# All matmuls at full 128x128 shape, and Q and K loaded four tokens per partition, in an attention and gated-unit kernel

## The chip, the cores and the metric

The kernel runs on one core of one Trainium2 chip. The metric is device time in microseconds (us) of one execution, lower is better. A core has a matrix engine (TensorE, PE in the profile, with its weight loads shown apart as PEld), a vector engine (VectorE, DVE), a scalar engine for activations (ScalarE, ACT), a general engine (GpSimd, POOL) and a queue engine that issues transfers (SyncE, SP). Each engine runs its own instructions in order; semaphores tie the engines together. SBUF is the on-chip memory, PSUM the memory that TensorE writes to.

## What is computed

Causal attention with a decay bias over 8 batches, 8 heads, 576 tokens and 64 dimensions a head, followed by a gated linear unit whose gate is a causal convolution of five taps.

```python
B, H, S, D = q.shape                                   # 8, 8, 576, 64
cum  = np.cumsum(np.maximum(s, 0.0), axis=-1)
bias = -(cum[:, :, :, None] - cum[:, :, None, :])
scores = np.matmul(q, k.transpose(0, 1, 3, 2)) / sqrt(D) + np.minimum(bias, 0.0)   # causal mask
attn = softmax(scores)
x = np.matmul(attn, v)                                 # to [B, S, 512]
gate = sigmoid(sum(conv_w[k] * x_shifted[k] for k in range(5)))
out = (gate * (x @ w_val)) @ w_out
```

## The kernel before

The bias splits into a factor per query, which the softmax normalisation cancels, and a factor per key, `w = exp(cum - half)`. It is multiplied into V, and a 65th column of V holds `w` itself, so that the same matmul also gives the softmax denominator. No maximum is subtracted. A small check on the denominators at the end decides whether a slower general path runs; with these inputs it doesn't.

576 tokens are four blocks of 128 and a tail block of 64 (`kbs`, `kbo`). Work goes by steps n: step n belongs to batch b = n / 4 and head pair p = n % 4, and a loop over n emits, with delays of one step or more, everything else:

- `load(b+1)` (L264), emitted at the first step of a batch: 15 transfers from HBM, for each token block Q, K and V in turn, every one in pieces of one token's 64 values (256 bytes). POOL casts Q and K to bf16 (L274) and multiplies V by `w` (L279, L281).
- `qk_transpose` (L286): five TensorE transposes of a 128-column slice into PSUM, the last of 64 tokens, and one DVE copy out (L294) to `QT` or `KT`, in which two heads lie one above the other, 64 partitions each.
- `scores4` (L296) and `scores` (L318): matmuls with 64 rows, one for each head, on partitions 0 to 63 and 64 to 127. ACT takes the exponential (L329), DVE masks the diagonal blocks (L332).
- `av` (L335): per head pair 30 matmuls of 65 columns; those for the tail queries have 64 columns of weights, those with the tail keys 64 rows. Two PSUM tiles, `psA` and `psB`, each evacuated by a reciprocal and a multiplication on DVE (L355, L356).
- `x_transpose` and `conv` (L360, L372): the result is transposed back (L368), copied by DVE (L370), and the five taps are one ACT instruction (L376), four DVE instructions (L378) and a tanh (L381).
- `val` and `outp` (L384, L397): the two products of the gated unit, four matmuls each, evacuated by DVE (L394) and ACT (L405).

A scheduler at build time puts the emitted instructions into an order for each engine, so that matmuls of different kinds stand mixed on TensorE. All transposes and both products of the gated unit share two PSUM buffers named `m` (pool `ps_m`); the scores have two of their own (`ps`). `qkst` and `vst` are the staging buffers of the transfers, four of each.

Of the kernel before, what the change touches and what calls it, by code (L numbers as in the profile page):

```python
# [206 lines left out]
def pcol(kb, qb):
    return DIAG[kb] if kb == qb else OFF0[kb] + kbo[qb]


def main_path(ctx, tc, q, k, v, s, moe_w_val, moe_conv_w, moe_w_out, out, okcnt):


    nc = tc.nc
# [34 lines left out]
    for i in range(NKB):  # L249
        n = kbs[i]  # L250
        pt = ps_m.tile([n, 64], FP32, name="m")
        nc.tensor.transpose(pt, cum[:, kbo[i]:kbo[i] + n], identf[0:64, 0:64])
        nc.scalar.activation(out=w[0:n, i, :], in_=pt, func=AF.Exp)

    recs = const_p.tile([128, B, 4, NKB, 2], FP32, name="recs")
    nc.vector.memset(recs, 1.0)
    psA = ps_av.tile([128, 3, 2, 65], FP32, name="psA")
    psB = ps_av.tile([128, 2, 2, 65], FP32, name="psB")
    nc.vector.memset(psB, 1.0)
# [4 lines left out]
    def load(b):  # L264
        qb_t = qkb_p.tile([128, NKB, 512], BF16, name="qb")
        kb_t = qkb_p.tile([128, NKB, 512], BF16, name="kb")
        Vp = v_p.tile([128, NKB, 8, 65], BF16, name="Vp")
        for i in range(NKB):
            n = kbs[i]
            for src, dst in ((q, qb_t), (k, kb_t)):  # L270
                st = stage_p.tile([128, 512], FP32, name="qkst")
                nc.sync.dma_start(out=st[0:n, :].rearrange("s (h d) -> s h d", h=8),
                                  in_=src[b, :, kbo[i]:kbo[i] + n, :].rearrange("h s d -> s h d"))
                nc.gpsimd.tensor_copy(dst[0:n, i, :], st[0:n, :])  # L274
            st = stage_p.tile([128, 512], FP32, name="vst")
            nc.sync.dma_start(out=st[0:n, :].rearrange("s (h d) -> s h d", h=8),
                              in_=v[b, :, kbo[i]:kbo[i] + n, :].rearrange("h s d -> s h d"))
            wb = w[0:n, i, b * 8:(b + 1) * 8]
            nc.gpsimd.tensor_tensor(Vp[0:n, i, :, 0:64], st[0:n, :].rearrange("s (h d) -> s h d", h=8),  # L279
                                    wb.unsqueeze(2).to_broadcast([n, 8, 64]), ALU.mult)  # L280
            nc.gpsimd.tensor_copy(Vp[0:n, i, :, 64:65], wb.unsqueeze(2))  # L281
        QT = qkt_p.tile([128, 4, S], BF16, name="QT")
        KT = qkt_p.tile([128, 4, S], BF16, name="KT")
        stage[b] = dict(qb=qb_t, kb=kb_t, Vp=Vp, QT=QT, KT=KT)

    def qk_transpose(b, p, which):  # L286
        st = stage[b]
        src, dst = (st["qb"], st["QT"]) if which == 0 else (st["kb"], st["KT"])
        pt = ps_m.tile([128, S], BF16, name="m")
        for i in range(NKB):  # L290
            n = kbs[i]
            nc.tensor.transpose(pt[:, kbo[i]:kbo[i] + n], src[0:n, i, p * 128:(p + 1) * 128],  # L292
                                ident[0:n, 0:n])
# [234 lines left out]
```

## Time and profile before

| | us |
|---|---|
| median of 3 runs | 349.25 |
| fastest and slowest of them | 346.63, 351.47 |
| the profiled execution | 348.8 |
| its span, first to last instruction | 347.2 |
| outside the span | 1.6 |

All durations are from the one profiled execution, so sums are made against its span of 347.2 us and the 1.6 us around it. An instruction group's line gives its source line, engine, operation, output and inputs by the program's names, shapes and count; behind the first bar the busy time and the mean duration of one in ns; behind the second the idle time of the engine just before, and who ended it. A matmul's shape is written rows*columns of the array that it uses, then the size of its streamed operand.

### The profile page before, as it was taken

How to read it: one execution, taken by the hardware profiler on the slowest of the kernel's cores; microseconds unless marked ns; L12 is line 12 of the kernel's file. 1: busy time of each engine (PE TensorE's matmuls, PEld its weight loads, DVE VectorE, ACT ScalarE, POOL GpSimd, SP SyncE). 2: the span in 40 equal slices, each digit the busy share in tenths (PEclk: the TensorE clock that was granted, in tenths of full speed). 3: DMA queues.
4: the chain of work that ended last, by engine and by line, in shares of the span. 5: the costliest groups of instructions: out<-in, count | busy, mean ns of one | idle time of the engine just before them, and what ended most of it. 6: DMA issues, size and time to landing. Idle time of an engine off the chain costs nothing.

```text
span 347.2 us, 6219 instructions
## 1 busy us (share of the span) xinstructions
PE 270.9 (78%) x2439; PEld 161.2 (46%) x2439; DVE 244.8 (70%) x466; ACT 168.7 (49%) x222; POOL 125.0 (36%) x179
## 2 busy tenths in 40 slices
PE   0236984878688798879997989889887998993990
PEld 0123652456345464556455535465554455561440
DVE  3023432774698789986989797968988789989740
ACT  0215740664248346932676263835484548741630
POOL 3661418760874017460558073803670000000000
PEclk9999999999999789955996798658995799696797
DMA  6995979971797007960499049912860030030322
GB/s 124 202 234 151 212 127 162 219 127 29 146 197 127 2 10 195 208 135 2 154 218 190 16 153 203 176 18 70 208 90 0 30 108 2 6 132 0 115 83 86
DMA packets 121910, 40.50 MB, mean 117 GB/s; under 512 B 116176, under 2 KB 116176, under 8 KB 121872
## 3 DMA queue, kind: packets, MB, share of 16 engines
q1 hardware_dynamic: 118992, 40.00, 56.6%
q10 hardware_dynamic: 2880, 0.01, 0.5%
q8 instruction: 21, 0.34, 0.5%
q14 instruction: 17, 0.14, 0.1%
HBM read 30.57 MB, written 9.44 MB: 115 GB/s over the span
## 4 chain that ended last, share of the span: by engine, by line
PE 41%; DVE 34%; ACT 10%; DMA 6%; issue 3%; POOL 3%; ACTq 1%; DVEq 0%; POOLq 0%
DVE gp L378 21%; PE m L392 9%; PE psB L349 8%; PE m L292 7%; PE ps L327 6%; ACT P L329 6%; PE psA L349 4%; DVE P L332 4%; PE m L368 4%; DMA cwT<-in_moe_conv_w_dram 3%; DVE glu L394 3%; PE m L402 2%; DVE xn L356 2%; DVE QT L294 1%; ACT gp L376 1%
## 5 line engine op out<-in xcount | busy, mean ns | idle before, releaser
L378 DVE SCALAR_TENSOR_TENSOR gp<-xT,cwT,gp 128x576 f32<-128x576 bf16 x128 | 118.0, 926 | 5.3 <-ACT gp L376 5.0
L329 ACT ACTIVATE P<-ps 128x1024 bf16<-128x1024 f32 x96 | 95.7, 1025 | 48.9 <-PE ps L327 48.6
L349 PEld LDWEIGHTS <-P 128*128 128x128 bf16 (+2 forms) x960 | 57.6, 118 | 37.2 <-issue 16.9
L327 PE MATMUL ps<-QT,KT 64*128 64x128 bf16 (+4 forms) x512 | 62.0, 297 | 12.8 <-ACT P L329 11.6
L279 POOL TENSOR_TENSOR Vp<-vst,w 128x512 bf16<-128x512 f32 (+1 forms) x40 | 52.9, 1322 | 28.0 <-DMA vst<-in_v_dram 21.3
L392 PE MATMUL m<-xT,wv 128*128 128x288 bf16 x256 | 51.0, 347 | 8.9 <-DVE xT L370 6.2
L349 PE MATMUL psB<-Vp,P 128*128 128x65 bf16 (+2 forms) x576 | 53.2, 226 | 5.3 <-DVE xn L356 3.9
L381 ACT ACTIVATE th<-gp 128x576 f32<-128x576 f32 x32 | 21.9, 684 | 48.4 <-DVE glu L394 48.2
L402 PE MATMUL m<-wo,glu 128*128 128x512 bf16 (+1 forms) x160 | 39.7, 389 | 0.2
L274 POOL CAST qb<-qkst 128x512 bf16<-128x512 f32 (+1 forms) x40 | 31.1, 779 | 21.6 <-DMA qkst<-in_q_dram 20.9
L392 PEld LDWEIGHTS <-wv 128*128 128x128 bf16 x256 | 26.4, 114 | 22.4 <-issue 12.3
L274 POOL CAST kb<-qkst 128x512 bf16<-128x512 f32 (+1 forms) x40 | 30.7, 769 | 16.1 <-DMA qkst<-in_k_dram 16.1
L294 DVE COPY QT<-m 128x576 bf16<-128x576 bf16 x32 | 14.5, 455 | 31.1 <-PE m L292 31.0
L327 PEld LDWEIGHTS <-KT 64*128 64x128 bf16 x512 | 24.5, 104 | 25.9 <-issue 18.7
L394 DVE SCALAR_TENSOR_TENSOR glu<-th,m 128x288 bf16<-128x288 f32 x64 | 28.7, 450 | 10.9 <-PE m L392 10.5
L376 ACT ACTIVATE gp<-xT,cwT 128x576 f32<-128x576 bf16 x32 | 24.9, 778 | 21.3 <-DVE xT L370 20.9
L292 PE MATMUL m<-ident,qb 128*128 128x128 bf16 (+1 forms) x160 | 24.2, 258 | 12.8 <-POOL qb L274 10.2
L405 ACT COPY ot<-m 128x512 f32<-128x512 f32 (+1 forms) x40 | 22.9, 583 | 22.8 <-PE m L402 20.4
L349 PE MATMUL psA<-Vp,P 128*128 128x65 bf16 x384 | 29.0, 220 | 5.2 <-DVE xn L356 2.2
L332 DVE TENSOR_TENSOR P<-P,tri 128x1024 bf16<-128x1024 bf16 x32 | 27.6, 861 | 2.0 <-ACT P L329 1.9
L292 PE MATMUL m<-ident,kb 128*128 128x128 bf16 (+1 forms) x160 | 23.8, 252 | 6.3 <-POOL kb L274 4.0
L368 PE MATMUL m<-ident,xn 128*128 128x128 bf16 (+1 forms) x160 | 20.7, 254 | 5.5 <-DVE QT L294 4.4
(45 smaller groups left out, 175.4 us busy)
## 6 DMA issues: line engine op xcount, KB each, us to landing
qkst<-in_q_dram SPq DMA_DIRECT2D x32, 256.0 KB, 4.6
qkst<-in_k_dram SPq DMA_DIRECT2D x32, 256.0 KB, 4.9
vst<-in_v_dram SPq DMA_DIRECT2D x32, 256.0 KB, 4.8
out_dram<-ot SPq DMA_DIRECT2D x32, 256.0 KB, 2.1
qkst<-in_q_dram SPq DMA_DIRECT2D x8, 128.0 KB, 5.1
qkst<-in_k_dram SPq DMA_DIRECT2D x8, 128.0 KB, 4.7
vst<-in_v_dram SPq DMA_DIRECT2D x8, 128.0 KB, 4.7
qkst<-in_moe_w_val_dram SPq DMA_DIRECT2D x4, 256.0 KB, 3.7
```

Of the source, the lines that this page charges most:

```text
L274: nc.gpsimd.tensor_copy(dst[0:n, i, :], st[0:n, :])
L279: nc.gpsimd.tensor_tensor(Vp[0:n, i, :, 0:64], st[0:n, :].rearrange("s (h d) -> s h d", h=8), wb.unsqueeze(2).to_broadcast([n, 8, 64]), AL ...
L292: nc.tensor.transpose(pt[:, kbo[i]:kbo[i] + n], src[0:n, i, p * 128:(p + 1) * 128], ident[0:n, 0:n])
L327: nc.tensor.matmul(ps[:, hh, c0:c0 + nq], st["KT"][r, p, kbo[kb]:kbo[kb] + 128], st["QT"][r, p, q0:q0 + nq], start=True, stop=True)
L329: nc.scalar.activation(out=Pt[:, :, step * 512:(step + 1) * 512], in_=ps, func=AF.Exp, scale=0.125)
L332: nc.vector.tensor_tensor(dg, dg, tri.unsqueeze(1).unsqueeze(1).to_broadcast([128, 2, 4, 128]), ALU.mult)
L349: nc.tensor.matmul(ps[0:nq, j, hh, :], lhsT, Vp[0:n, kb, 2 * p + hh, :], start=(kb == 0), stop=(kb == qb))
L368: nc.tensor.transpose(pt[:, kbo[i]:kbo[i] + n], st["xn"][0:n, i, p * 128:(p + 1) * 128], ident[0:n, 0:n])
L378: nc.vector.scalar_tensor_tensor(gp, xc[:, kk:kk + S], cwT[:, c * 5 + kk:c * 5 + kk + 1], gp, ALU.mult, ALU.add)
L392: nc.tensor.matmul(psv, wv[:, dc, c * 128:(c + 1) * 128], st["xT"][:, dc, 4 + o:4 + o + 288], start=(dc == 0), stop=(dc == 3))
L394: nc.vector.scalar_tensor_tensor(st["glu"][:, c, o:o + 288], st["th", c][:, o:o + 288], 1.0, psv, ALU.add, ALU.mult)
L402: nc.tensor.matmul(pso, st["glu"][:, c, kbo[i]:kbo[i] + nq], wo[:, c, :], start=(c == 0), stop=(c == 3))
```

## The change

Every matmul uses the full 128x128 array. The Q of two heads is kept in two tiles `QZ`, each zero in the other head's 64 partitions, so that both heads use the same 128-partition K slice as weights. The tail block of 64 tokens becomes a window of 128 (tokens 448 to 575): weights, score columns and the masked `P4` are arranged so that the first 64 rows add nothing, and only the last 64 are stored.

The first 512 tokens of Q and K come in one transfer a batch each (two for the first batch), with four successive tokens of a head on one partition, so that a piece is 1,024 bytes; the last 64 tokens of both come as a `tail` tile. The transposes then give tokens in the order (token mod 4, token / 4). K is put back in order when ACT copies it out of PSUM. Q is permuted within each 128-block by two DVE copies of 64 partitions; its order stays interleaved through the scores and the second matmul, and the DVE copy after `x_transpose` puts it back. `psA` and `psB` become one tile `psav` with one reciprocal and one multiplication for both heads.

The emission order changes too: `load_qk(b+2)` stands after the last step of batch b, V is loaded after the first, `x_transpose` and `conv` come ahead of the transposes of the next batch, `val` is two items, and the output products are spread over four steps.

```diff
 def load_qk(b):                                    # was: load(b)
+        for r, src in ((slice(0, 64), q), (slice(64, 128), k)):
+            nc.sync.dma_start(out=tail[r, :].rearrange("s (h d) -> s h d", h=8),
+                              in_=src[b, :, 512:576, :].rearrange("h s d -> s h d"))
+        nc.gpsimd.tensor_copy(tailb, tail)
...
+        parts = [(0, 2), (2, 8)] if b == 0 else [(0, 8)]
+        for h0, h1 in parts:
+            for src, f, t in ((q, qf, qb), (k, kf, kb)):
+                nc.sync.dma_start(out=f[:, h0:h1, :],
+                                  in_=src[b, h0:h1, 0:512, :].rearrange("h (p j) d -> p h (j d)", j=4))
+                nc.gpsimd.tensor_copy(
+                    t.rearrange("p j (h d) -> p h j d", h=8)[:, h0:h1],
+                    f.rearrange("p h (j d) -> p h j d", j=4)[:, h0:h1])
...
+        if which == 0:
+            for hh in range(2):
+                r = slice(64 * hh, 64 * hh + 64)
+                nc.vector.tensor_copy(st["QZ"][hh][r, p, 0:512].rearrange("d (i j r) -> d j i r", j=4, i=4),
+                                      pt[r, :].rearrange("d (j i r) -> d j i r", j=4, i=4))
+        else:
+            nc.scalar.copy(st["KT"][:, p, 0:512].rearrange("d (x j) -> d x j", j=4),
+                           pt.rearrange("d (j x) -> d x j", j=4))
-        nc.vector.tensor_copy(dst[:, p, :], pt)
...
-                r = slice(64 * hh, 64 * hh + 64)
-                nc.tensor.matmul(ps[:, hh, c0:c0 + nq], st["KT"][r, p, kbo[kb]:kbo[kb] + 128],
-                                 st["QT"][r, p, q0:q0 + nq], start=True, stop=True)
+                nc.tensor.matmul(ps[:, hh, c0:c0 + nq], st["KT"][:, p, kbo[kb]:kbo[kb] + 128],
+                                 st["QZ"][hh][:, p, q0:q0 + nq], start=True, stop=True)
...
+        pv = psav[:, :, 0:325].rearrange("t h (g d) -> t h g d", d=65)
+        rec = recs[:, b * 4 + p]
+        nc.vector.reciprocal(rec, pv[:, :, :, 64])
...
-        nc.vector.tensor_copy(st["xT"][:, p, 4:4 + S], pt)
+        nc.vector.tensor_copy(
+            st["xT"][:, p, 4:516].rearrange("d (i r j) -> d i r j", i=4, j=4),
+            pt[:, 0:512].rearrange("d (i j r) -> d i r j", i=4, j=4))
+        nc.vector.tensor_copy(st["xT"][:, p, 516:4 + S], pt[:, 512:S])
...
+        nc.gpsimd.memset(d["QZ"][0][64:128], 0.0)
+        nc.gpsimd.memset(d["QZ"][1][0:64], 0.0)
+        nc.gpsimd.memset(d["P4"], 0.0)
...
-        for c in range(4):
-            wt = stage_p.tile([128, DM], FP32, name="qkst")
-            nc.sync.dma_start(out=wt, in_=src[c * 128:(c + 1) * 128, :])
+        wt = qkf_p.tile([128, 4, DM], FP32, name="qkf")
+        nc.sync.dma_start(out=wt, in_=src.rearrange("(c p) d -> p c d", c=4))
```

The queue of SyncE at the program's start, before: transfers of Q, K and V of the first batch in turn, block by block (`qkst`, `vst`), then the weights.

```order
L243 DMA sp<-in_s_dram 64x576
L272 DMA qkst<-in_q_dram 128x8x64
L272 DMA qkst<-in_k_dram 128x8x64
L276 DMA vst<-in_v_dram 128x8x64
L272 DMA qkst<-in_q_dram 128x8x64
...
L276 DMA vst<-in_v_dram 64x8x64
L415 DMA qkst<-in_moe_w_val_dram 128x512 x4
```

The same place now; `qkf` is the staging tile of Q and K, with three buffers that the weights share.

```order
L301 DMA tail<-in_q_dram 64x8x64
L301 DMA tail<-in_k_dram 64x8x64
L312 DMA qkf<-in_q_dram 128x2x256
L312 DMA qkf<-in_k_dram 128x2x256
L312 DMA qkf<-in_q_dram 128x6x256
L312 DMA qkf<-in_k_dram 128x6x256
L323 DMA vst<-in_v_dram 128x8x64 x4
L323 DMA vst<-in_v_dram 64x8x64
L463 DMA qkf<-in_moe_w_val_dram 128x4x512
```

All of Q and K of the first batch now stands ahead of its V, and the weights behind both as before.

VectorE where the first convolution begins, before: `QT` and `KT` are copies for the second batch, `xT` and `gp` belong to the first batch's convolution.

```order
L294 COPY QT<-m 128x576 x2
L294 COPY KT<-m 128x576 x2
L294 COPY QT<-m 128x576
L294 COPY KT<-m 128x576
L370 COPY xT<-m 128x576
L294 COPY QT<-m 128x576
L294 COPY KT<-m 128x576
L378 SCALAR_TENSOR_TENSOR gp<-xT,cwT,gp 128x576
```

The same place now, with the two half-tiles of Q by their numbers.

```order
L350 COPY QZ_157<-m 64x4x4x32
L350 COPY QZ_158<-m 64x4x4x32
L403 RECIPROCAL recs<-psav 128x10
L404 TENSOR_TENSOR xn<-psav,recs 128x2x5x64
L416 COPY xT<-m 128x512
L419 COPY xT<-m 128x64
L350 COPY QZ_157<-m 64x4x4x32
L350 COPY QZ_158<-m 64x4x4x32
L427 SCALAR_TENSOR_TENSOR gp<-xT,cwT,gp 128x576
```

The K copies are gone from this engine, each Q copy is two, the copy of `xT` is two; the first `gp` still stands behind three of the four Q copies of the second batch.

## Rows read from the trace of the kernel before

**Rows 1.** The page's busy times: engine, busy us, share of the span, instructions.
```profile
PE 270.9 (78%) x2439; PEld 161.2 (46%) x2439; DVE 244.8 (70%) x466; ACT 168.7 (49%) x222; POOL 125.0 (36%) x179
```

**Rows 2.** Busy time by stage: stretch, length, engines with counts, granted clock, DMA share, GB/s.
```profile
0.00:26.00 26.00, 5.88 (x33) 3.23 (x33) 4.90 (x11) 3.45 (x8) 14.44 (x39) 1.00 0.99 186
26.00:64.00 38.00, 29.05 (x266) 17.65 (x264) 14.01 (x33) 15.98 (x20) 15.73 (x25) 1.00 0.87 168
125.00:298.00 173.00, 153.15 (x1432) 90.27 (x1433) 147.97 (x272) 100.05 (x130) 66.28 (x83) 0.81 0.52 110
```

**Rows 3.** Busy time by stage, single stretches of 20 us, same columns.
```profile
220.00:240.00 20.00, 18.97 (x161) 11.46 (x161) 16.39 (x31) 9.60 (x13) 8.08 (x9) 0.59 0.31 62
300.00:320.00 20.00, 14.19 (x129) 8.68 (x130) 18.72 (x40) 6.85 (x11) 0.00 (x0) 0.84 0.17 60
```

**Rows 4.** The end of the program, all engines in order of time.
```profile
333.83 1.02 DVE L394 SCALAR_TENSOR_TENSOR glu<-th,m 128x288 bf16<-128x288 f32 x2 [0.17 <-PE m L392]
334.34 4.61 PE L402 MATMUL m<-wo,glu 128*128 128x512 bf16 x20
```

**Rows 5.** TensorE in order of time, at a granted clock of 1.00.
```profile
196.29 0.23 PE L327 MATMUL ps<-QT,KT 64*128 64x128 bf16 x2
196.45 0.53 PE L368 MATMUL m<-ident,xn 128*128 128x128 bf16 x5
...
197.47 1.15 PE L392 MATMUL m<-xT,wv 128*128 128x288 bf16 x8
```

**Rows 6.** TensorE in order of time, at a granted clock of 0.50.
```profile
186.97 0.61 PE L327 MATMUL ps<-QT,KT 64*128 64x448 bf16 x4
...
192.03 2.08 PE L392 MATMUL m<-xT,wv 128*128 128x288 bf16 x8 [0.49 <-DVE xT L370]
```

**Rows 7.** Instruction groups of VectorE, by shape, whole span.
```profile
L378 DVE SCALAR_TENSOR_TENSOR gp<-xT,cwT,gp 128x576 f32<-128x576 bf16 x128 | 118.0, 926 | 5.3 <-ACT gp L376 5.0
L332 DVE TENSOR_TENSOR P<-P,tri 128x1024 bf16<-128x1024 bf16 x32 | 27.6, 861 | 2.0 <-ACT P L329 1.9
L356 DVE TENSOR_TENSOR xn<-psA,recs 128x384 bf16<-128x384 f32 x32 | 17.6, 551 | 0.3
L294 DVE COPY QT<-m 128x576 bf16<-128x576 bf16 x32 | 14.5, 455 | 31.1 <-PE m L292 31.0
L356 DVE TENSOR_TENSOR xn<-psB,recs 128x256 bf16<-128x256 f32 x32 | 13.3, 417 | 0.3
L355 DVE RECIPROCAL recs<-psA 128x6 f32<-128x6 f32 x32 | 6.0, 188 | 12.1 <-PE psA L349 12.1
L355 DVE RECIPROCAL recs<-psB 128x4 f32<-128x4 f32 x32 | 5.5, 172 | 6.6 <-PE psB L349 6.5
```

**Rows 8.** Instruction groups of VectorE from 298 to 347 us, where POOL is idle.
```profile
L378 DVE SCALAR_TENSOR_TENSOR gp<-xT,cwT,gp 128x576 f32<-128x576 bf16 x24 | 19.5, 815 | 2.5 <-ACT gp L376 2.3
L332 DVE TENSOR_TENSOR P<-P,tri 128x1024 bf16<-128x1024 bf16 x2 | 1.4, 687 | 0.0
```

**Rows 9.** Instruction groups of POOL, by shape, whole span.
```profile
L279 POOL TENSOR_TENSOR Vp<-vst,w 128x512 bf16<-128x512 f32 x32 | 42.6, 1331 | 27.7 <-DMA vst<-in_v_dram 21.3 <-issue 3.4 <-PE psB L349 1.9
L274 POOL CAST qb<-qkst 128x512 bf16<-128x512 f32 x32 | 24.3, 758 | 21.6 <-DMA qkst<-in_q_dram 20.9
L364 POOL MEMSET xT<- 128x16 bf16 x8 | 0.8, 110 | 62.4 <-issue 24.1 <-ACT P L329 19.5 <-PE m L392 18.8
masks.py:197 POOL MEMSET ident<- 128x128 bf16 x1 | 0.2, 205 | 0.3 <-POOLq L512 0.3
```

**Rows 10.** The start, in order of time: first cast on POOL, two exponentials of the first batch.
```profile
5.30 0.89 POOL L274 CAST qb<-qkst 128x512 bf16<-128x512 f32 x1 [3.50 <-DMA qkst<-in_q_dram]
...
30.77 1.01 ACT L329 ACTIVATE P<-ps 128x1024 bf16<-128x1024 f32 x1
...
47.95 1.02 ACT L329 ACTIVATE P<-ps 128x1024 bf16<-128x1024 f32 x1 [1.11 <-PE ps L327]
```

**Rows 11.** The line of `gp`: count, shortest, median and longest ns, first and last start.
```profile
L378 DVE SCALAR_TENSOR_TENSOR gp<-xT,cwT,gp x128: 773/814/1852, 64.5 to 330.1; 128x576 f32<-128x576 bf16 x128
```

More of the change, by code (lines that the diff above doesn't have):

```diff
@@ L249, in main_path @@
     for i in range(NKB):
[L250 to L259, printed above, removed]
-    stage = {}
@@ L264, in load @@
[L264 to L267, printed above, removed]
+        pt = ps_m.tile([128, 64], FP32, name="m")
+        nc.tensor.transpose(pt, cum[:, WIN[i]:WIN[i] + 128], identf[0:64, 0:64])
+        nc.scalar.activation(out=w[:, i, :], in_=pt, func=AF.Exp)
+    recs = const_p.tile([128, B * 4, 2, NKB], FP32, name="recs")
+    psav = ps_av.tile([128, 2, 512], FP32, name="psav")
@@ L268, in load, with load_v @@
+    def load_v(b):
+        Vp = sets[b % 2]["Vp"]
         for i in range(NKB):
             n = kbs[i]
[L270 to L275, printed above, removed]
@@ L283, in load, with tail_transpose @@
-        KT = qkt_p.tile([128, 4, S], BF16, name="KT")
-        stage[b] = dict(qb=qb_t, kb=kb_t, Vp=Vp, QT=QT, KT=KT)
+            nc.sync.dma_start(out=vst[128 - n:128, i, :, 0:64],
+                              in_=v[b, :, kbo[i]:kbo[i] + n, :].rearrange("h s d -> s h d"))
+            nc.gpsimd.tensor_tensor(Vp[:, i], vst[:, i],
+                                    w[:, i, b * 8:(b + 1) * 8].unsqueeze(2).to_broadcast([128, 8, 65]),
+                                    ALU.mult)
+    def tail_transpose(b):
+        st = stage[b]
+        pt = ps_m.tile([128, 4, 128], BF16, name="m")
+        for p in range(4):
+            nc.tensor.transpose(pt[:, p, :], st["tail"][:, p * 128:(p + 1) * 128], ident)
+        for hh in range(2):
+            r = slice(64 * hh, 64 * hh + 64)
+            nc.vector.tensor_copy(st["QZ"][hh][r, :, 512:S], pt[r, :, 0:64])
+        nc.scalar.copy(st["KT"][:, :, 512:S], pt[:, :, 64:128])
@@ L286, in qk_transpose @@
     def qk_transpose(b, p, which):
         st = stage[b]
[L288 to L293, printed above, removed]
-        nc.vector.tensor_copy(dst[:, p, :], pt)
+        c = slice(p * 128, (p + 1) * 128)
+        pt = ps_m.tile([128, 512], BF16, name="m")
@@ new lines, in qk_transpose @@
+        for j in range(4):
+            nc.tensor.transpose(pt[:, j * 128:(j + 1) * 128], st["qk"][which][:, j, c], ident)
+        if which == 0:
+            for hh in range(2):
+                r = slice(64 * hh, 64 * hh + 64)
+                nc.vector.tensor_copy(st["QZ"][hh][r, p, 0:512].rearrange("d (i j r) -> d j i r", j=4, i=4),
[3 more added lines that the diff above has]
+                           pt.rearrange("d (j x) -> d x j", j=4))
@@ L424, in main_path @@
         qk_transpose(0, p, 1)
+    load_qk(1)
     NS = B * 4
-    for n in range(NS + 9):
+    OUTS = [(0, 1), (2,), (3,), (4,)]
+    for n in range(NS + 12):
         b, p = divmod(n, 4)
-        if p == 0 and b + 1 < B:
-            load(b + 1)
         fill = []
```

183 lines of the change are left out of this document (102 added, 81 removed), and 6 rows, old and new, of the table STEPS.

## The prediction

> **What bounds the kernel now.** I read the page's busy times first, then the same by stage, then the groups of the engine that looks fullest, then a few stretches of TensorE in order of time. No engine is full over the span: PE is busy 270.9 us of 347.2, DVE 244.8 [rows 1]. The stages tell more [rows 2]. Up to 64 us the transfers bound: the DMA share is 0.99 and then 0.87, DVE has worked only 4.90 + 14.01 us, and the first `gp`, the convolution that makes up nearly half of DVE's work, starts at 64.5 [rows 11]. From 125 to 298 us two engines are nearly full at once: PE 153.15 of 173 us (88.5%), DVE 147.97 (85.5%). At the end DVE is alone, 18.72 of 20 us [rows 3]; its last `glu` ends at 334.85, then come twenty matmuls, copies and stores up to 347.2, 12.3 us [rows 4].
>
> So three things can change the time: when DVE gets its main work, how much work it has, and how often it waits for PE. I take DVE's work as the bound and ask for these three.
>
> **PE: what goes, what comes.** A change of array shape costs TensorE time. At full clock the pair of 64*128 matmuls at 196.29 is followed by the next shape 0.16 us later [rows 5], though 128 columns stream in 0.055 us: the eight matmuls of 288 columns in 1.15 us give about 0.123 us each [rows 5]. I call a change 0.1 us. Per head pair the code has some 16 of them: two around each of the three transposes' short fifth block, two around each of three score groups, four in the tail of `av`; the scheduler's mixing adds some, and following the matmul starts through the trace I count 570. That is 57 us of PE, all of which goes.
>
> In return the two heads no longer share the array. At half clock, four matmuls of 448, 448, 64 and 64 columns take 0.61 us [rows 6]. One after another, 1024 columns at 1.2 GHz would be 0.85 us, as pairs 0.43 us and the last one's run out: they run as pairs. After the change each group streams all 1024, and a head pair has three such groups: 1536 columns more, times 32, is 49,000, 20.5 us at 2.4 GHz. In the trace 180 of 288 possible pairs run together, so the loss lies between 13 and 21 us; I take 16. PE thus loses about 40 of its 271 us. It is a partner of DVE in the middle, so this is no saving in itself; it lets DVE wait less.
>
> Here a rule of the Trainium skill speaks against the change: TensorEngine Tiling (Array Packing), sections Theoretical Speedup and Performance Considerations, holds that a contraction of 64 should use two row tiles, worth up to twice the speed. The pairs above agree with it. By that rule alone the change would add 20 us to PE and save nothing. The same page says under Key Properties that a change of tiling mode drains the engine; the 0.16 us step agrees, and in this mixed order that side is the larger.
>
> **DVE: the work.** Removed, 32 of each [rows 7]: copies of QT, KT and xT (0.455 each, 1.365), two reciprocals (0.360), two multiplications for `xn` (0.968), together 2.69 us, 86.1 us. Added:
> - 64 copies of Q, 512 elements on 64 partitions, runs of 32. Bounds: 0.40, the QT row scaled to 512 elements, and 0.685, the rate of the `xn` rows (551 - 417 for 128 elements is 1.047 ns each; 417 + 256 x 1.047). Source, type and unit step are those of the QT row, so I take 0.43: 27.5 us (25.6 to 43.8).
> - 32 copies of xT, 512 elements read with a step of 32, and 32 of 64 elements. No row reads PSUM so. Same bounds; I take the upper one, 0.685, because the step is unlike the QT row, and 0.19 for the short one as for a reciprocal: 28.0 us (18 to 28).
> - one `xn` of 640 elements: 551 + 256 x 1.047 = 819 ns, 26.2 us; one reciprocal of 10: 188 + 4 x 8 = 220 ns, 7.0 us.
> - 16 tail copies of 256 elements, between 0.2 (the QT row scaled) and 0.417: 0.3, 4.8 us.
>
> That is 93.5 us, 7.4 more (from -5 to +24). K's copies go to ACT, 32 of about 0.6 us; ACT is busy 168.7 us [rows 1] and has room.
>
> DVE also loses time to POOL. `gp` takes 926 ns on average and 815 with POOL idle, the mask 861 and 687 [rows 7, 8]: 128 x 0.111 + 32 x 0.174 = 19.8 us, for 125.0 us of POOL. Now POOL has 40 products for V at 1.33 us [rows 9], 53 us, eight tail casts at 0.76, 6 us, and 16 casts of 2048 elements; these cost at least one small cast, 0.76, at most four, 3.0, and I take 2.4: 38 us. That is 97 us, 28 less, so DVE gets back 4.4 us. DVE's work becomes 244.8 + 7.4 - 4.4 = 248 us (235 to 268).
>
> On the first of these copies the Trainium skill, VectorE: DVE Perf Modes, section What auto-detection actually checks, gives two elements a cycle only to 16-bit operands of unit step. By it Q stays fast and xT slows, the values that I took; no row here shows the strided one.
>
> **When DVE gets its work.** Before, the first cast starts at 5.30 and the first masked exponential at 30.77 [rows 10]. Now POOL first clears four tiles of 2304 elements and two of 1024. Two fills give 0.85 ns an element (205 - 110 over 112) [rows 9], so 2.05 us and 0.97 us each, 10.1 us; with the small ones the first cast comes at 13 us. Tail, two heads and six heads of Q and K take some 6 us, to 19; copies out add 3: first exponential at about 22. Six of the twelve exponentials of a batch (30.77 to 47.95 for the first [rows 10], 1.43 us each) bring us to 31. The first `gp` still stands behind Q copies of the second batch; its K needs the third staging buffer, which the cast of the first weight frees at about 25, then a megabyte of transfer, a cast, transposes and copies: I take 38 us, within 33 to 45. DVE has then done about 15 us.
>
> **The sum.** From 38 us DVE has 248 - 15 = 233 us left. The share of time in which it works was 85.5% beside a full PE and 93.6% in the best late stretch [rows 2, 3]; with PE 40 us lighter I take 91%: 256 us, to 294. The end stays 12.3: span 306.3, with the 1.6 us outside it 308 us, against 348.8 for the profiled execution and 349.25 for the median. Own range: 289 (start 35, 226 us left, 94%) to 330 (start 42, 240 left, 88%, is 329).
>
> **Rivals.**
> - *The Q copies run at one element a cycle.* 64 x 0.255 = 16.3 us more DVE work, at 91% 18 us: 326. For it: four-dimensional patterns, which no row shows. Against: they keep the unit step of the QT row.
> - *The waits stay.* The two `m` buffers still serve all transposes and products, now 6.5 tiles a step; `psav` is one tile for both heads, so `av` waits for the whole `xn` before it. Then DVE stays at 85.5%: 233 / 0.855 = 272.5, total 324.
> - *The early start does not come.* The transfers of the second batch queue behind V and weights, and ten us of clearing stand in front of the first cast. If the convolution starts at 64 as before, with 20 us done: 64 + 228 / 0.91 + 13.9 = 328.
> - *Slower: TensorE's clock.* The granted clock is 0.81 from 125 to 298 us and 0.59 in one stretch of 20 us [rows 2, 3], and the 288-column products take 2.08 instead of 1.15 us at half clock [rows 5, 6]. After the change PE streams 378,000 columns (960 x 65, 102,000 for scores, 448 transposes x 128, 256 x 288, 160 x 512): 157 us at 2.4 GHz, 315 at 1.2. If the clock fell to 1.2 GHz for good, PE would bound: 22 + 315 / 0.95 + 8 = 362. It decides from a mean clock of about 0.57 down. For it: zero rows, no pairs, less to do. Against: an engine that falls behind is never idle, and at 0.59 PE was busy 18.97 of 20 us and came back.
>
> **How the numbers follow.** My forecast 0.57, Q copies 0.14, waits 0.13, late start 0.08, clock 0.06, and 0.02 for several of the first three together, which meet the old time. About 2% is what a measurement of this kernel can tell from no change: 342 to 356 us. The first four cases lie below it, less some combinations: faster 0.88, same 0.07, slower 0.05. The range 288 to 340 leaves out most of the clock's case, the combinations, and the forecast's far ends.
>
> **What would show it.** Right: no row with 64 rows or 64 columns of the array except at the very start; PE near 230 us busy; DVE near 248; Q copies at 0.43 and xT at 0.69; first `gp` near 38 us; DVE over 90% busy in the middle. Wrong: a first `gp` after 50 us, Q copies over 0.6, a granted clock under 0.6 on average, or a DVE share of 85% with PE waiting on `m`.

## The result, and the profile after

The changed kernel takes 312.02 us (median of 4 runs, 308.75 to 312.78), the kernel before 349.48 beside it (346.63 to 351.47): ratio 0.892, 95% interval 0.883 to 0.901, so 10 to 12% less time. The forecast was 308 (288 to 340). The profiled execution took 312.78 us, its span is 311.1.

The page's busy times, to be laid beside [rows 1]:

```profile
PE 215.4 (69%) x2384; PEld 151.6 (49%) x2407; DVE 259.6 (83%) x456; ACT 186.4 (60%) x256; POOL 107.0 (34%) x88
```

PE works 55.5 us less, DVE 14.8 us *more*, ACT 17.7 more, POOL 18.0 less. The kernel is faster although DVE, the engine that bounds it, has more to do. By stage, with the columns of [rows 2]:

```profile
0.00:24.00 24.00, 8.09 (x58) 5.48 (x58) 9.66 (x17) 4.70 (x10) 22.84 (x31) 1.00 0.89 212
24.00:45.00 21.00, 14.14 (x201) 11.43 (x202) 10.41 (x19) 17.74 (x20) 11.27 (x11) 0.76 1.07 281
45.00:75.00 30.00, 20.08 (x245) 15.22 (x243) 29.17 (x43) 20.56 (x28) 14.77 (x9) 0.72 1.02 260
100.00:258.00 158.00, 121.30 (x1418) 86.82 (x1435) 150.59 (x273) 106.08 (x147) 45.38 (x29) 0.92 0.34 95
```

From 45 us on DVE is full (29.17 of 30 us, later 150.59 of 158, 95%), and PE is its partner no longer: 121.30 of 158 us, 77%, where [rows 2] had 88.5%. VectorE's groups, to be laid beside [rows 7]:

```profile
L427 DVE SCALAR_TENSOR_TENSOR gp<-xT,cwT,gp 128x576 f32<-128x576 bf16 x128 | 123.7, 967 | 3.8 <-ACT gp L425 3.6
L442 DVE SCALAR_TENSOR_TENSOR glu<-th,m 128x288 bf16<-128x288 f32 x64 | 28.6, 448 | 6.6 <-PE m L440 6.1
L382 DVE TENSOR_TENSOR P<-P,tri 128x1024 bf16<-128x1024 bf16 x32 | 26.9, 841 | 2.8 <-ACT P L379 2.0
L350 DVE COPY QZ<-m 64x512 bf16<-64x512 bf16 x64 | 26.8, 419 | 5.1 <-PE m L346 4.4
L404 DVE TENSOR_TENSOR xn<-psav,recs 128x640 bf16<-128x640 f32 x32 | 26.1, 815 | 0.1
L416 DVE COPY xT<-m 128x512 bf16<-128x512 bf16 x32 | 21.4, 668 | 0.7 <-PE m L415 0.7
L366 DVE TENSOR_TENSOR P<-P,tri 128x512 bf16<-128x512 bf16 x8 | 8.0, 1003 | 7.3 <-ACT P L364 7.3
L403 DVE RECIPROCAL recs<-psav 128x10 f32<-128x10 f32 x32 | 6.8, 213 | 0.2
L419 DVE COPY xT<-m 128x64 bf16<-128x64 bf16 x32 | 5.7, 179 | 0.0
```

The last column counts idle time: the waits of [rows 7] before the copies of QT (31.1 us) and the reciprocals (12.1 and 6.6) have fallen to 5.1 (`QZ`) and 0.2 us. The copies cost what they were priced at; `gp` rose from 926 to 967 ns.

To weigh this I cut each trace at two marks, the first `gp` and the last `glu`. Between them DVE's records are joined into busy time; that over the time between the marks is its share, and span = first `gp` + busy / share + end:

| | first `gp` | DVE busy between | share | end | span |
|---|---|---|---|---|---|
| before | 64.5 | 225.3 | 0.834 | 12.3 | 347.2 |
| forecast | 38 | 233 | 0.91 | 12.3 | 306.3 |
| after | 45.6 | 238.9 | 0.945 | 12.7 | 311.1 |

From before to after: start 18.9 us earlier; fuller DVE 225.3 x (1/0.834 - 1/0.945) = 31.7 us saved; more work 13.6/0.945 = 14.4 us paid. Seen by batches (every sixteenth `gp` begins one): the first six took 34.7 to 41.9 us each before and take 31.8 to 33.9 now, together 223.8 and 199.8 us; the last two, where DVE was alone before too, take 53.0 instead of 46.5.

### The profile page after: what moved, and what is told of

Read it like the earlier page. It is cut to its first block, busy times and chain, and to the rows that moved or that the text cites. A ratio compares the mean times of both kernels' runs of the same rounds, so it can differ in the third digit from the quotient of the medians.

```text
span 311.1 us, 6044 instructions
## 1 busy us (share of the span) xinstructions
PE 215.4 (69%) x2384; PEld 151.6 (49%) x2407; DVE 259.6 (83%) x456; ACT 186.4 (60%) x256; POOL 107.0 (34%) x88
## 5 line engine op out<-in xcount | busy, mean ns | idle before, releaser
L427 DVE SCALAR_TENSOR_TENSOR gp<-xT,cwT,gp 128x576 f32<-128x576 bf16 x128 | 123.7, 967 | 3.8 <-ACT gp L425 3.6
L379 ACT ACTIVATE P<-ps 128x1024 bf16<-128x1024 f32 x96 | 96.7, 1025 | 27.1 <-PE ps L377 24.2
L377 PE MATMUL ps<-QZ,KT 128*128 128x128 bf16 (+4 forms) x512 | 75.8, 273 | 16.9 <-ACT P L379 15.1
L314 POOL CAST qkb<-qkf 128x2048 bf16<-128x2048 f32 (+2 forms) x18 | 32.9, 1843 | 98.2 <-issue 44.1
L377 PEld LDWEIGHTS <-KT 128*128 128x128 bf16 x512 | 43.4, 110 | 32.4 <-issue 22.9
L395 PE MATMUL psav<-Vp,P 128*128 128x65 bf16 x960 | 43.6, 201 | 21.0 <-DVE xn L404 18.1
L325 POOL TENSOR_TENSOR Vp<-vst,w 128x520 bf16<-128x520 f32 x40 | 55.2, 1412 | 0.0
L395 PEld LDWEIGHTS <-P 128*128 128x128 bf16 x960 | 39.5, 103 | 27.7 <-issue 16.3
L440 PE MATMUL m<-xT,wv 128*128 128x288 bf16 x256 | 46.5, 314 | 7.1 <-DVE xT L419 4.4
L450 PE MATMUL m<-wo,glu 128*128 128x512 bf16 x137 | 40.2, 388 | 13.7 <-DVE glu L442 11.8
L453 ACT COPY ot<-m 128x512 f32<-128x512 f32 (+1 forms) x40 | 23.4, 585 | 37.0 <-PE m L450 35.0
L346 PE MATMUL m<-ident,qkb 128*128 128x128 bf16 x256 | 28.0, 242 | 6.9 <-DVE xT L419 3.3
L350 DVE COPY QZ<-m 64x512 bf16<-64x512 bf16 x64 | 26.8, 419 | 5.1 <-PE m L346 4.4
L404 DVE TENSOR_TENSOR xn<-psav,recs 128x640 bf16<-128x640 f32 x32 | 26.1, 815 | 0.1
L346 PEld LDWEIGHTS <-qkb 128*128 128x128 bf16 x256 | 19.4, 108 | 12.7 <-issue 7.5
```

The costliest lines, as they stand in the source:

```text
L325: nc.gpsimd.tensor_tensor(Vp[:, i], vst[:, i], w[:, i, b * 8:(b + 1) * 8].unsqueeze(2).to_broadcast([128, 8, 65]), ALU.mult)
L346: nc.tensor.transpose(pt[:, j * 128:(j + 1) * 128], st["qk"][which][:, j, c], ident)
L350: nc.vector.tensor_copy(st["QZ"][hh][r, p, 0:512].rearrange("d (i j r) -> d j i r", j=4, i=4), pt[r, :].rearrange("d (j i r) -> d j i r", ...
L377: nc.tensor.matmul(ps[:, hh, c0:c0 + nq], st["KT"][:, p, kbo[kb]:kbo[kb] + 128], st["QZ"][hh][:, p, q0:q0 + nq], start=True, stop=True)
L379: nc.scalar.activation(out=Pt[:, :, step * 512:(step + 1) * 512], in_=ps, func=AF.Exp, scale=0.125)
L395: nc.tensor.matmul(psav[:, hh, qb * 65:qb * 65 + 65], lhsT, Vp[:, kb, 2 * p + hh, :], start=(kb == 0), stop=(kb == qb))
```

## The experiments

Each is the changed kernel with the edit shown, the main lines of it alone (`...` marks what is left out); ratios are to the kernel before in the same series, 0.892 being the changed kernel. Differences in us compare series in which the kernel before took 347.97 to 350.44 us, so one or two us between two runs decide nothing.

**Scores alone back on 64 rows.**

```diff
-                nc.tensor.matmul(ps[:, hh, c0:c0 + nq], st["KT"][:, p, kbo[kb]:kbo[kb] + 128],
-                                 st["QZ"][hh][:, p, q0:q0 + nq], start=True, stop=True)
+                r = slice(64 * hh, 64 * hh + 64)
+                nc.tensor.matmul(ps[:, hh, c0:c0 + nq], st["KT"][r, p, kbo[kb]:kbo[kb] + 128],
+                                 st["QZ"][hh][r, p, q0:q0 + nq], start=True, stop=True)
```

> Changed kernel with the scores alone back at 64 rows: the same QZ and KT tiles, sliced to each head's 64 partitions, so that two heads run as a pair and every score group is a change of array shape again. Theory (changes of shape cost about 0.1 us of PE each, but VectorE bounds and hides most of it): some 8 changes a head pair, 256 in all, 26 us of PE more, 16 us less by the pairs, so PE +10 us and the time +0 to +5 us, 312 to 317. Rival A (each change of shape is on the path): +20 us or more, 332. Rival B (the pairs are worth more than the changes cost, row tiling pays): 296 to 306.

314.48 us, ratio 0.899 (0.894 to 0.903): 2.5 us more, at the edge of the intervals. The groups of 128 and 448 columns, in the changed kernel:

```profile
L377 PE MATMUL ps<-QZ,KT 128*128 128x128 bf16 x256 | 30.9, 247 | 4.6 <-ACT P L379 2.8 <-ACT P L364 1.1
L377 PE MATMUL ps<-QZ,KT 128*128 128x448 bf16 x64 | 22.0, 391 | 0.0
```

the same two with 64 rows:

```profile
L378 PE MATMUL ps<-QZ,KT 64*128 64x128 bf16 x256 | 23.4, 252 | 4.2 <-ACT P L380 2.1 <-ACT P L364 1.4
L378 PE MATMUL ps<-QZ,KT 64*128 64x448 bf16 x64 | 18.6, 407 | 0.0
```

and the page's busy times of that run:

```profile
PE 217.1 (69%) x2384; PEld 137.4 (44%) x2407; DVE 258.7 (83%) x456; ACT 186.0 (60%) x256; POOL 107.5 (34%) x88
```

Two heads side by side save PE time in the scores (30.9 to 23.4 us, 22.0 to 18.6; 17.9 us over all five groups), yet PE as a whole is busy 217.1 us against 215.4: 262 shape changes, counted through the trace, take back what the pairs give. The Trainium skill, TensorEngine Tiling (Array Packing), Performance Considerations, asks for two row tiles at a contraction of 64; this run agrees that the pair is cheaper by itself, and shows that in a mixed order it gains nothing.

**All old shapes** (scores, `scores4`, tail queries and keys of `av`, output tail).

```diff
...
-                nc.tensor.matmul(psav[:, hh, qb * 65:qb * 65 + 65], lhsT, Vp[:, kb, 2 * p + hh, :],
+                rk = slice(64, 128) if kb == 4 else slice(0, 128)
+                rq = slice(64, 128) if qb == 4 else slice(0, 128)
+                nc.tensor.matmul(psav[rq, hh, qb * 65:qb * 65 + 65], lhsT[rk, rq], Vp[rk, kb, 2 * p + hh, :],
...
```

> Changed kernel with the array shapes of before for scores (64 rows), tail scores, tail queries and tail keys of the second matmul and the tail of the output product (64 columns), the loads, the order of emission and the copies as changed. Theory: 10 to 13 changes of shape a head pair, 330 to 420 in all, PE +20 to +26 us net, VectorE's share of time back towards 88 to 90%: 322 to 330 us. Rival A (shapes are nearly all of the gain): 342 to 349. Rival B (the loads, the order and the early start are the gain, shapes don't matter): 309 to 315.

332.6 us, 0.948 (0.941 to 0.954): 20.6 us more, a little over the forecast for it. Busy times of the page, then the stretch from 100 to 258 us:

```profile
PE 247.6 (75%) x2389; PEld 152.2 (46%) x2407; DVE 257.3 (78%) x457; ACT 188.9 (57%) x256; POOL 104.9 (32%) x88
```

```profile
100.00:258.00 158.00, 133.13 (x1307) 81.36 (x1319) 137.25 (x249) 99.14 (x134) 49.80 (x34) 0.79 0.38 103
```

PE 32.2 us busier, DVE's share 0.876 instead of 0.945, its work between the marks 4.4 us less. Of the 20.7 us by which the span grew, 14.8 are this link from shapes to time through DVE's waits (234.5/0.876 - 238.9/0.945); the first `gp` comes 4.0 us later (49.6), the end is 1.9 us longer. The granted clock fell too, from 0.92 to 0.79 in this stretch, but single executions at like clocks over the whole span stay as far apart: 329.29 us at 0.908 with the old shapes beside 311.37 at 0.907, and 333.12 at 0.896 beside 312.67 at 0.897. So the clock is not what makes the old shapes slow.

**xT copied by ACT** (both copies).

```diff
...
-        nc.vector.tensor_copy(st["xT"][:, p, 516:4 + S], pt[:, 512:S])
+        nc.scalar.copy(st["xT"][:, p, 516:4 + S], pt[:, 512:S])
```

> Changed kernel with both copies of xT moved from VectorE to ScalarE, 27.1 us of VectorE work (32 x 0.668 and 32 x 0.179 us) off, about the same on ScalarE, which is busy 186 of 311 us. Theory (VectorE's work is the bound): the time falls by 24 to 28 us, 284 to 290. Rival (the two shared PSUM buffers and TensorE are as near as VectorE): less than half of it, 300 to 308. Rival (ScalarE's in-order queue makes xT late): 312 or more.

293.94 us, 0.842 (0.838 to 0.847): 18 us less than the changed kernel. DVE's busy time between the marks falls by 21.0 us to 217.9, less than the 27.1 of the two groups since neighbouring records overlap; the share falls to 0.930. So DVE's work is the bound. The time lies between the forecast (284 to 290) and the rival (300 to 308), and decides for the first in kind only.

**The start's clears of both `QZ` and `P4` on DVE, a fourth staging buffer.**

```diff
-    qkf_p = P("qkf", 3)
+    qkf_p = P("qkf", 4)
...
-        nc.gpsimd.memset(d["QZ"][0][64:128], 0.0)
+        nc.vector.memset(d["QZ"][0][64:128], 0.0)
...
```

> Changed kernel with the six clearing fills at the start (QZ, P4) on VectorE, which is idle there, in place of POOL, and four staging buffers of Q and K in place of three. POOL's first cast should come at 5 to 6 us in place of 14.2, and the staging of the second batch no longer waits for the first weight's cast. Theory (clearing and staging set the start): first gp from 45.6 to about 36 us and the time 8 us less, 302 to 306. Rival (the transfers set the start: DMA share 1.07 between 24 and 45 us): 309 to 313.

310.78 us, 0.889 (0.885 to 0.892). The first cast comes at 5.8 instead of 14.2 us, the first `gp` at 47.9, no earlier. The ten us of clearing, and the third buffer, are not what holds the start.

**The weight casts later.**

```diff
-        nc.scalar.activation(out=dst, in_=wt, func=AF.Copy, scale=sc)
+        late.append((dst, wt, sc))
...
+        if n in (1, 2):
+            dst, wt, sc = late[n - 1]
+            nc.scalar.activation(out=dst, in_=wt, func=AF.Copy, scale=sc)
```

> The changed kernel with one thing moved: the two weight casts on ACT (1.91 us each, the first waiting 3.42 us for its transfer) are emitted after the second and third step of the main loop instead of ahead of the first K copies; a fourth staging buffer keeps their data meanwhile. Theory (ACT's in-order queue holds the start: K copies of batch 0 stand behind a cast that waits): first gp from 45.6 to about 40 us, time 306 to 308 against 312. Rival (the transfers of the second batch, or the pipeline's own depth, hold the first gp): first gp stays within 2 us of 45.6 and the time within 3 us of 312.

311.04 us, 0.894 (0.881 to 0.908); first `gp` 43.9. This did not test it: in ACT's order the cast of `wv` still ran at 23.73, ahead of a K copy at 25.55. The run with three edits, below, does.

**Pieces of 256 bytes**, one transfer for each `j` of four.

```diff
-                nc.sync.dma_start(out=f[:, h0:h1, :],
-                                  in_=src[b, h0:h1, 0:512, :].rearrange("h (p j) d -> p h (j d)", j=4))
+                for j in range(4):
+                    nc.sync.dma_start(out=f[:, h0:h1, j * 64:(j + 1) * 64],
+                                      in_=src[b, h0:h1, 0:512, :].rearrange("h (p j) d -> p j h d", j=4)[:, j])
```

> The changed kernel with Q and K read in pieces of 256 bytes (four transfers of each megabyte, one per token of the four) instead of 1 KB; the place in SBUF and all that follows is the same. Before and after differ by 49,985 packets and 795 us of packet time summed over 16 engines, some 3.1 us for each of 16 megabyte transfers. Theory (the pieces matter at the start alone): first gp 6 to 12 us later, 52 to 58 us, then everything is hidden again, time 318 to 325. Rival (the early start comes from elsewhere, the pieces are hidden everywhere): 310 to 315, first gp as in the changed kernel.

315.12 us, 0.906 (0.888 to 0.923), single runs 312.69, 312.91, 317.34 and 321.54: without the last their median is 312.91, as the rival said. It is not told apart from the changed kernel; the cost is 0.9 to 3.1 us. The first `gp` did move to 51.7; in that trace DVE then had less to do (`gp` 934 ns), and its span was 311.1 all the same.

**The old order of steps** (`x_transpose` and `conv` behind the next batch's transposes as well).

```diff
...
-            fill += [lambda: val(b3, c3, 0), lambda: val(b3, c3, 1)]
...
-            fill += [lambda i=i: outp(b4, i) for i in OUTS[c4]]
+            fill += [lambda: (val(b3, c3, 0), val(b3, c3, 1))]
+            if c3 == 3:
+                fill += [lambda i=i: outp(b3, i) for i in range(NKB)]
```

> The changed kernel with the old order of the steps in the main loop: transposes of Q and K of the next batch ahead of the transpose of x and the convolution, both halves of the value product as one step, all five output blocks at the end of a batch instead of four steps later. Shapes, copies and loads stay new. Theory (DVE's share of time between first gp and last glu, 0.945, comes from the order as well as from the shapes; old shapes in the new order gave 0.876, the kernel before 0.834): share 0.89 to 0.92, time 318 to 328. Rival (shapes are all of it): share 0.94, 310 to 314.

314.82 us, 0.904 (0.894 to 0.914), share 0.929. The theory wanted 318 to 328: missed. Alone the order is worth 2 to 3 us.

**Without 30 of the 40 V products.**

```diff
-            nc.gpsimd.tensor_tensor(Vp[:, i], vst[:, i],
+            if b < 2:
+              nc.gpsimd.tensor_tensor(Vp[:, i], vst[:, i],
...
```

> The changed kernel without 30 of POOL's 40 V products (those of batches 2 to 7; these batches use the weighted V of the first two, the V transfers stay): this part of the computation is left out. It takes 42 us of POOL's 107 away and nothing else. Theory (POOL at work slows DVE: gp 808 ns with POOL idle, near 1490 beside it, 967 on average): gp mean near 880 to 910, DVE 8 to 13 us less busy, time 299 to 305. Rival (gp's spread comes from something else, or the gain goes into waits): 309 to 314.

292.86 us, 0.841 (0.832 to 0.850), 19 us less, more than the theory asked. Busy times of the page (of the longest of six runs, 296.49 us), then two groups of VectorE:

```profile
PE 210.7 (71%) x2407; PEld 147.7 (50%) x2407; DVE 245.8 (83%) x456; ACT 185.5 (63%) x256; POOL 63.9 (22%) x58
```

```profile
L428 DVE SCALAR_TENSOR_TENSOR gp<-xT,cwT,gp 128x576 f32<-128x576 bf16 x128 | 114.3, 894 | 2.4 <-ACT gp L426 1.8
...
L367 DVE TENSOR_TENSOR P<-P,tri 128x512 bf16<-128x512 bf16 x8 | 3.3, 416 | 7.0 <-ACT P L365 7.0
```

POOL works 43.1 us less and DVE, whose instructions are the same, 13.8 us less: 0.32 us of DVE for one of POOL. `gp` falls from 967 to 894 ns, the mask of L366 from 1003 to 416.

**Three edits together:** xT on ACT, late weight casts, clears on DVE with the fourth buffer.

```diff
...
+        nc.vector.memset(d["QZ"][0][64:128], 0.0)
...
+        nc.scalar.copy(st["xT"][:, p, 516:4 + S], pt[:, 512:S])
...
+        late.append((dst, wt, sc))
...
```

> Three edits on the changed kernel together: both xT copies on ACT (alone 293.9), the weight casts after the second and third step with a fourth staging buffer (alone 311.0), the start's clears of QZ and P4 on DVE (alone, with the fourth buffer, 310.8). Theory (the gains add): 289 to 292, first gp at or before 44 us. Rival (with DVE lighter, PE and ACT set the pace and an earlier start is waited away): 293 to 296.

294.0 us, 0.844 (0.838 to 0.849): no faster than xT on ACT alone, as the rival said. But now the cast is out of the way. ACT and POOL at the start, in order of time:

```profile
21.54 1.03 ACT L379 ACTIVATE P<-ps 128x1024 bf16<-128x1024 f32 x1
23.25 1.02 ACT L379 ACTIVATE P<-ps 128x1024 bf16<-128x1024 f32 x1 [0.21 <-PE ps L377]
...
26.79 1.91 ACT L513 ACTIVATE wv<-qkf 128x2048 bf16<-128x2048 f32 x1
...
35.19 1.90 POOL L314 CAST qkb<-qkf 128x2048 bf16<-128x2048 f32 x1 [2.56 <-DMA qkf<-in_k_dram]
```

The exponentials run on from 21.5 us, and still the first `gp` is at 47.9. The second batch's K cast waits for its transfer until 35.19. In the changed kernel, with the issue of that transfer on SyncE:

```profile
20.01 1.02 ACT L379 ACTIVATE P<-ps 128x1024 bf16<-128x1024 f32 x1
24.46 1.91 ACT L464 ACTIVATE wv<-qkf 128x2048 bf16<-128x2048 f32 x1 [3.42 <-DMA qkf<-in_moe_w_val_dram]
...
26.39 0.79 SPq L312 DMA_DIRECT2D qkf<-in_k_dram  x1
...
27.22 1.04 ACT L379 ACTIVATE P<-ps 128x1024 bf16<-128x1024 f32 x1
...
35.11 1.90 POOL L314 CAST qkb<-qkf 128x2048 bf16<-128x2048 f32 x1 [1.25 <-DMA qkf<-in_k_dram]
```

With the fourth buffer the transfer is issued from 22.82 us on and lands no earlier. Over nine kernels with the new shapes that cast starts between 34.1 and 42.6 us and the first `gp` comes 9.2 to 12.7 us behind it. So the transfers of the second batch set when the start can come, as far as these runs tell; they aren't all of it, for with the old shapes `gp` follows 13.0 us behind, and with old shapes and old order 19.0 (34.6 and 53.6 us).

**The same, and twelve large casts on ACT**, emitted one and two steps after their transfers.

```diff
-                nc.gpsimd.tensor_copy(
+                eng = nc.gpsimd.tensor_copy if b < 2 else nc.scalar.copy
...
-        if p == 3 and b + 2 < B:
+        if p == 1 and b + 2 < B:
             load_qk(b + 2)
+        if p >= 2 and casts:
+            casts.pop(0)()
```

> As the run with the three edits, and from the third batch on the twelve large casts of Q and K (2.07 us each on POOL, 25 us) on ACT, their transfers issued two steps earlier. Theory (each us of POOL work costs DVE about a third of a us: 42 us less POOL gave 13.8 us less DVE work and 19 us less time): DVE 6 to 9 us less busy than with the three edits, time 280 to 286. Rival (a cast disturbs DVE less than the V product does, or ACT, then near 235 us busy, becomes the bound): no gain, or slower.

296.38 us, 0.852 (0.848 to 0.856): no gain on the three edits. Busy times of the page, then the groups of `gp` and `glu`:

```profile
PE 212.7 (72%) x2384; PEld 149.3 (50%) x2407; DVE 229.9 (78%) x398; ACT 223.3 (75%) x332; POOL 68.1 (23%) x70
```

```profile
L433 DVE SCALAR_TENSOR_TENSOR gp<-xT,cwT,gp 128x576 f32<-128x576 bf16 x128 | 109.7, 860 | 4.4 <-ACT gp L431 3.6
L448 DVE SCALAR_TENSOR_TENSOR glu<-th,m 128x288 bf16<-128x288 f32 x64 | 28.7, 450 | 18.1 <-PE m L446 17.3
```

Half of the theory holds (9.6 us less DVE work between the marks, `gp` 860 ns), but the share falls from 0.928 to 0.879. What POOL no longer took from DVE came back as waits, above all that of `glu` for its TensorE product (17.3 us, 8.0 with the three edits), with ACT at 223.3 us; that ACT, in TensorE's way, is behind them is the likely reading, not a tested one.

**Three old parts at once: shapes, small pieces, order** (the edits above).

```diff
...
+                                      in_=src[b, h0:h1, 0:512, :].rearrange("h (p j) d -> p j h d", j=4)[:, j])
...
+                nc.tensor.matmul(psav[rq, hh, qb * 65:qb * 65 + 65], lhsT[rk, rq], Vp[rk, kb, 2 * p + hh, :],
...
+            fill += [lambda: (val(b3, c3, 0), val(b3, c3, 1))]
...
```

> The changed kernel with three of its parts put back at once: array shapes of before in the scores, the tail of av and the output (alone 332.6), Q and K in pieces of 256 bytes (alone 315.1), the old order of steps (alone 314.8). Theory (the parts add): 332.6 + 3.1 + 2.8, so 335 to 342, and the other 8 to 14 us to the kernel before lie in the rest (K copies on ACT, one xn and reciprocal for both halves, loads a batch ahead). Rival (the parts bite only together, when PE is full): 345 to 355, as before.

349.18 us (10 runs), 1.004 (0.9995 to 1.009): the whole gain is gone. It isn't the kernel before again: the first `gp` comes 10.2 us earlier (54.3 for 64.5), and DVE has 9.6 us more work between the marks at much the same share (0.844 for 0.834). The two nearly cancel.

**Shapes and order, pieces of 1 KB.**

```diff
...
+                nc.tensor.matmul(psav[rq, hh, qb * 65:qb * 65 + 65], lhsT[rk, rq], Vp[rk, kb, 2 * p + hh, :],
...
+            fill += [lambda: (val(b3, c3, 0), val(b3, c3, 1))]
...
```

> The changed kernel with the old array shapes and the old order of steps, Q and K still in pieces of 1 KB. Old shapes alone gave 332.6; shapes, order and 256-byte pieces together gave 349.2, as slow as the kernel before, where the sum of the single effects would be 338.5. Theory (the order bites beside a fuller PE: DVE's share .876 falls to about .845): 341 to 346. Rival (the order is worth 2 to 3 us here too, and the small pieces bite): 334 to 338.

337.22 us, 0.967 (0.953 to 0.980). Both from 100 to 258 us, first with the three parts:

```profile
100.00:258.00 158.00, 125.50 (x1250) 77.47 (x1253) 132.92 (x234) 93.64 (x129) 50.99 (x34) 0.81 0.54 116
```

and then with shapes and order alone:

```profile
100.00:258.00 158.00, 128.70 (x1320) 80.31 (x1318) 139.42 (x246) 98.70 (x135) 46.20 (x31) 0.83 0.36 101
```

The theory wanted 341 to 346 and missed; the rival was within 334 to 338. The order adds 4.6 us to the old shapes, near its 2.8 alone. The small pieces add 12 us here (333.5 to 339.0 us without them, 347.1 to 351.9 with them) and 0.9 to 3.1, not told from nothing, in the changed kernel. They hurt DVE's share (0.864 to 0.844) at the same work, and the start is much the same (53.6 and 54.3). Why they cost so much beside old shapes and old order, and next to nothing beside the new ones, is open, and so is which of the two it takes: neither was run with them alone. With small pieces the large casts wait for their transfers in both cases (54.7 us on POOL beside the new, 49.2 beside the old, 7.4 in the changed kernel), so that wait alone does not tell. Nor does a fuller PE: from 100 to 258 us it is busy 125.50 us with the three parts, less than the 133.13 with the old shapes alone.

## Why the prediction was right, and where its steps were off

**The mechanism held.** DVE bounds (18 us for taking its xT copies away), PE's shape changes made it wait (20.6 us for putting the old shapes back, 14.8 of them by DVE's share), and both changes of the start and of the share came. The rivals: *Q copies at one element a cycle* falls, 419 ns. *The waits stay* falls, share 0.945. *The early start does not come* falls in the main, 45.6 and not 64. *TensorE's clock* falls: the granted clock rose from 0.81 [rows 2] to 0.92 in the middle, with PE less busy.

Three steps were off, and they nearly cancel, so that the sum came within 4 us is luck in part: from the forecast span of 306.3, the start +7.6, the work +5.9/0.91 = +6.5, the share 238.9 x (1/0.945 - 1/0.91) = -9.7, the end +0.4, is 311.1.

- *First `gp` at 38 us.* It came at 45.6. The first cast (14.2 for 13) was right, the first exponential came even earlier (20.0 for 22). Wrong was "six of the twelve exponentials bring us to 31": the next one came at 27.2, behind the weight's cast. More than that, what I named last set the time: the second batch's K, whose transfer I let start at about 25. It is issued at 26.4, nearly so; but its cast waits for it until 35.1, and 10.5 us of transposes, copies and steps follow. My 38 left 13 us for what took 19.
- *DVE's work, 248 us.* Measured 259.6. The added copies, `xn` and reciprocals were right to 2 us: Q 26.8 (27.5), xT 27.1 (28.0), `xn` 26.1 (26.2), reciprocals 6.8 (7.0), tails 4.5 (4.8). The failed step is "DVE gets back 4.4 us" from a lighter POOL. POOL is lighter (107.0 for 125.0, ten us of it clearing before DVE's work begins), but `gp` costs 123.7 us against 118.0, and the eight masks of the tail keys (L366) take 8.0 us, for which the kernel before needed 4.6:

```profile
L307 DVE TENSOR_TENSOR P<-P,tri 64x512 bf16<-64x512 bf16 x8 | 4.6, 571 | 1.1 <-ACT P L305 1.1
```

  The price per us of POOL was no constant. With POOL idle the rows are, from 258 to 298 us:

```profile
L427 DVE SCALAR_TENSOR_TENSOR gp<-xT,cwT,gp 128x576 f32<-128x576 bf16 x24 | 19.4, 810 | 0.4 <-ACT gp L425 0.4
L442 DVE SCALAR_TENSOR_TENSOR glu<-th,m 128x288 bf16<-128x288 f32 x20 | 8.9, 447 | 3.7 <-PE m L440 3.7
...
L382 DVE TENSOR_TENSOR P<-P,tri 128x1024 bf16<-128x1024 bf16 x3 | 2.0, 681 | 0.0
```

  So 128 x 157 ns + 32 x 160 = 25.2 us of slowing, for the 72.9 us that POOL works after 45 us: 0.35. Before it was 19.8 for the 94.8 after 64 us [rows 1, 2]: 0.21. (The small masks add 8 x 587 ns, 1003 - 416, that is 4.7 us, now.) A fuller DVE that meets POOL more often is not the reason: by the records, `gp` overlaps 54.6 us of POOL's work before and 41.8 now, 58% of what POOL works after the first `gp` both times. What rose is the price of an overlapped us, from 0.26 (14.2 us) to 0.48 (20.1 us). In the run without V products nearly all that overlaps `gp` are the casts of 2048 elements, at 0.66 (10.8 us for 16.4); in the one with twelve casts on ACT nearly all are V products, at 0.35 (6.4 for 18.1). Before, over half of the overlap, 30.9 us, were casts of 512 elements or less. So the large casts, which I priced by POOL's time alone, are the likely reason; no run changes their size by itself.
- *A share of 91%.* It was 0.945. PE fell by 55.5 us and not by 40, which is enough to account for it: on a straight line from the run with the old shapes, PE 247.6 and share 0.876, to the changed kernel, 215.4 and 0.945, the forecast's 231 lies at 0.91 (an estimate). The two terms of the 40 were sized well. The five groups of scores lose 17.9 us by running one after another, within the 13 to 21. A change of shape can be priced from the starts of all matmuls of the kernel before: at a granted clock of 1.00 the next one starts 0.055 us (median of 377) behind one of 128 columns where its shape is the same, 0.152 (of 116) where it isn't; behind one of 65 columns it is 0.036 and 0.145, and at 0.50 0.055 and 0.176. That is 0.10 to 0.12 us a change, where I took 0.1. By these PE would have fallen 39 to 45 us (an estimate; a quarter of the changes stand at 0.50). The other ten or more stand in neither term, and that is what the 40 had wrong. Part may be the clock, 0.92 for 0.81: the value product, whose shape did not change, fell from 51.0 to 46.5 us. No run separates it.

What a sum can't show: the parts are not additive. Old shapes +20.6, old order +2.8, small pieces +0.9 to +3.1, together 24 to 27; put back together they cost 37.2, as much as the whole gain. Nearly all of the difference is the small pieces beside the other two, 12 us; shapes and order nearly add (25.2 for 23.4). Of the 18.9 us by which DVE starts earlier, 8.7 go with the three parts; what brings the other ten, no run took out.

## What to carry to other kernels

Where two engines are nearly full together, taking work from the one that doesn't bound can pay, through the waits of the one that does (the new shapes alone brought DVE's share from 0.876 to 0.945). A part that is worth 1 to 3 us alone can be worth 12 beside two others: put parts back together, not only singly. Price a mixed order of array shapes by its changes, not by what each shape gains. Price the work that one engine does by what it costs another too, and by its kind: POOL's large casts cost `gp` about twice what its V products did. Then look at the engine that bounds: moving xT's copies to ACT, one call in two places, gave 18 us more (293.9 us; the three edits, at 294.0, are level with it, and no kernel that computes everything is faster), and the next move, casts onto ACT, gave nothing.

## What the runs showed of the hardware that was not expected

POOL slows some of DVE's instructions and leaves others alone. `gp` takes 810 ns with POOL idle and 1631 in a stretch where POOL worked 6.69 of 7 us (86 to 93 us of the changed kernel); `glu` beside it is unmoved:

```profile
86.00:93.00 7.00, 3.17 (x32) 2.02 (x31) 7.00 (x7) 2.54 (x3) 6.69 (x5) 0.97 0.76 171
```

```profile
L427 DVE SCALAR_TENSOR_TENSOR gp<-xT,cwT,gp 128x576 f32<-128x576 bf16 x4 | 6.5, 1631 | 0.0
L442 DVE SCALAR_TENSOR_TENSOR glu<-th,m 128x288 bf16<-128x288 f32 x2 | 0.9, 440 | 0.0
L366 DVE TENSOR_TENSOR P<-P,tri 128x512 bf16<-128x512 bf16 x1 | 0.8, 823 | 0.0
```

Slow are the two masks and `gp`, which read two tensors from SBUF; the copies, `xn` and `glu`, which read PSUM, keep their times (`xn` 815 ns over the whole span, 818 with POOL idle). The Trainium skill, SBUF — State Buffer, section Who interferes with whom, says just this: with two SBUF inputs a DVE instruction contends with a GpSimd one that reads SBUF, with at most one, outside DVE's 2-port modes, it does not. The rows agree. It works the other way too: the V product takes 1055 ns where no `gp` or mask overlaps it (4 of the 40) and 1452 where one does (the other 36), 1412 on average.

```profile
L325 POOL TENSOR_TENSOR Vp<-vst,w 128x520 bf16<-128x520 f32 x40 | 55.2, 1412 | 0.0
```

The granted clock in the middle was 0.92 in the changed kernel, 0.79 with the old shapes, 0.83 with shapes and order, 0.81 with all three parts. It does not simply follow PE's busy time: of these 158 us PE was busy 121.30, 133.13, 128.70 and 125.50. No run holds the clock fixed; the executions at like clocks, under the old shapes above, show that the gain of the shapes doesn't hang on it.
